# Threshold attention with a feed-forward block on one core: nine slots of 256 queries a batch, FFN by 288 tokens, scores in six shared PSUM banks, variance by a broadcast product

## Chip, cores, metric

One core of one Trainium2 chip. The metric is device time in microseconds (us) of one execution. The kernel before takes 1555.65 us, the median of 3 runs (1554.12 to 1557.59). Ratios are the mean time of one kernel's fast runs over that of the other's fast runs in the same rounds, so they are not quite the ratio of the medians quoted beside them; 95% intervals are in brackets.

The engines are called PE (TensorE; PEld its weight loads), DVE (VectorE), ACT (ScalarE), POOL (GpSimd) and SP (SyncE, which issues most transfers).

## The reference, cut

```python
# q, k, v: (8, 8, 576, 64) float32; tau = 0.02; w_ch1: 512 x 2048; w_ch2: 2048 x 512 (float64)
scores = np.matmul(q, k.transpose(0, 1, 3, 2)) / np.sqrt(64)
thresh = np.max(scores, -1, keepdims=True) - tau
scores = np.where(scores >= thresh, scores, -1e9)
attn   = softmax(scores)                       # (written out in the original)
x      = (attn @ v).transpose(0, 2, 1, 3).reshape(8, 576, 512)
mu, var = x.mean(-1), x.var(-1)                # per token
xn     = (x - mu) / np.sqrt(var + 1e-6) * g_ln
out    = x + np.maximum(xn @ w_ch1, 0) @ w_ch2
```

A *unit* below is one pair of heads of one batch. "em" is the transposed attention weights, "hidden" the output of the first FFN product after its ReLU, "o" an output tile of the second.

## The kernel before, what matters

All products are float32. A unit is worked off in five points: four of 128 queries of both heads, and one that holds the 64 queries of both that are left, through a block-diagonal stationary operand. Each side of a point has a PSUM tile of its own, from a pool that turns over two:

```python
scs = [ps_sc.tile([128, 2, 512], F32, tag="sc", name="sc") for _ in sides]   # ps_sc: bufs=2
...
for i, sc in enumerate(scs):                     # exponentials
    nc.vector.tensor_reduce(out=neg[:, i:i+1], in_=sc[:, :, :HALF], op=ALU.max, negate=True, ...)
    nc.gpsimd.tensor_scalar(out=thr[:, i:i+1], ...)
    nc.scalar.activation(es[:, i]..., sc[:, :, :HALF], func=AF.Exp, bias=neg[:, i:i+1])
...
for i, sc in enumerate(scs):                     # weights: multiply by (score >= threshold)
    nc.vector.scalar_tensor_tensor(out=e2, in0=sc[:, :, :HALF], scalar=thr[:, i:i+1], in1=e2, ...)
```

The FFN goes by nine groups of 512 tokens. Each output tile of it takes a PSUM bank of a pool of two, and ACT (first product) or DVE (second) empties it. The DVE multiply is put in a list, `aside`, which is issued after the point's threshold multiplies:

```python
for m in range(NK):
    p2 = ps_ff.tile([128, TOK], F32, tag="ff", name="p2")
    for d in range(ND):
        product(p2, lhsT=w2_sb[d][:, m*128:(m+1)*128], rhs=hidden[:, d], ...)
    aside.append(lambda m=m, p2=p2: add_to_x(g, m, p2, rb))    # o = p2 * rb, then + x
...
scs = scores(u, j);  es, thr = exponentials(scs);  conversion.carry()
run(3 * n);  second_part(n, 0)          # FFN products, a share of the open group
weights(scs, es, thr);  run_aside()
conversion.end();  run(3 * n + 1);  second_part(n, 1)
```

The float64 weights are turned into float32 on the fly in the first points (`conversion`): work for DVE, ACT and POOL.

Of the kernel before, what the change touches and what calls it, by code (L numbers as in the profile page):

```python
# [18 lines left out]
def kernel(  # L19
# [24 lines left out]

    nc = tc.nc
    B, H, S, D = q.shape
    DM = H * D
    DF = w_ch1.shape[1]
    assert (S, D, DM) == (576, 64, 512) and DF % 128 == 0
# [4 lines left out]
    PTS = J + 1  # L54
    NB = S // 32
    HALF = S // 2
    SCALE = 1.0 / 8.0
    BIG = 3.0e38
    TOK = 512
    NG = B * S // TOK  # L60
    assert NG * TOK == B * S

    consts = ctx.enter_context(tc.tile_pool(name="consts", bufs=1))
    ins = ctx.enter_context(tc.tile_pool(name="ins", bufs=2))
# [3 lines left out]
    xpool = ctx.enter_context(tc.tile_pool(name="xpool", bufs=3))  # L68
    ps_sc = ctx.enter_context(tc.tile_pool(name="ps_sc", bufs=2, space=bass.MemoryType.PSUM))
    ps_at = ctx.enter_context(tc.tile_pool(name="ps_at", bufs=2, space=bass.MemoryType.PSUM))  # L70
    ps_ff = ctx.enter_context(tc.tile_pool(name="ps_ff", bufs=2, space=bass.MemoryType.PSUM))

    ffn = ctx.enter_context(tc.tile_pool(name="ffn", bufs=4))
# [10 lines left out]
    q_diag = [consts.tile([128, 128], F32, name=f"q_diag{i}") for i in range(2)]  # L84
    v_rest = [consts.tile([128, 2, D], F32, name=f"v_rest{i}") for i in range(2)]
# [30 lines left out]
    def load_v(u):  # L116
        b, hp = units[u]
        vt = ins.tile([128, J, 2, D], F32, tag="v", name="v_in")
        vr = v_rest[u % 2]
        for h in range(2):  # L120
            nc.sync.dma_start(  # L121
                out=vt[:, :, h, :],
                in_=v[b, 2 * hp + h, : J * 128, :].rearrange("(c p) d -> p c d", p=128),
            )
            nc.sync.dma_start(out=vr[64 * h : 64 * h + 64, h, :], in_=v[b, 2 * hp + h, J * 128 :, :])  # L125
        values_in[u] = (vt, vr)
# [5 lines left out]
    for t in v_rest:  # L132
        nc.gpsimd.memset(t, 0.0)
    for t in q_diag:
        nc.gpsimd.memset(t, 0.0)
    load_qk(0, (nc.sync, nc.scalar))
# [19 lines left out]

    hidden = consts.tile([128, ND, TOK], F32, name="hidden")

    def weight_steps(which):
# [10 lines left out]
        if which == 1:  # L170
            chunks = [
                (w1_sb[i][:, c : c + WC], w_ch1[i * 128 : (i + 1) * 128, c : c + WC], i)
                for c in range(0, DF, WC)
                for i in range(NK)
            ]
        else:
            chunks = [
                (w2_sb[i], w_ch2[i * 128 : (i + 1) * 128, :], None) for i in range(ND)
            ]
        size = len(chunks)  # L180
        step = 4 if which == 1 else 2
        place = [ND - step * ((i % 4 if which == 1 or i < size - 4 else i % 2) + 1) for i in range(size)]
        raws, made = {}, {}

        def fetch_raw(i):
            at = place[i]
            raws[i] = hidden[:, at : at + 2].rearrange("p a n -> p (a n)").bitcast(I64)
            nc.sync.dma_start(out=raws[i], in_=chunks[i][1])

        def begin(i):  # L190
            if which == 1:
                a, y = hidden[:, place[i] + 2], hidden[:, place[i] + 3]
            else:
                a = ffn.tile([128, WC], F32, tag="o", name="w_bits")
                y = ffn.tile([128, WC], F32, tag="o", name="w_size")
            raw = raws.pop(i)
            words = raw.bitcast(U32).rearrange("p (n two) -> p n two", two=2)
            lo, hi = words[:, :, 0], words[:, :, 1]
            r = raw.bitcast(I32).rearrange("p (n two) -> p n two", two=2)[:, :, 0]
            au = a.bitcast(U32)  # L200
# [8 lines left out]
            nc.scalar.activation(r, lo, func=AF.Copy, scale=2.0**-29)  # L209
            nc.scalar.activation(  # L210
                y, raw.bitcast(F32).rearrange("p (n two) -> p n two", two=2)[:, :, 1],
                func=AF.Square,
            )
            made[i] = (a, y, r)

        def carry(i):
            a, y, r = made[i]
            ai = a.bitcast(I32)
            nc.gpsimd.tensor_tensor(out=ai, in0=ai, in1=r, op=ALU.add)
            if place[i] in place[i + 1 :]:  # L220
                fetch_raw(place.index(place[i], i + 1))

        def end(i):
            a, y, r = made.pop(i)
            dst, _, gi = chunks[i]
# [4 lines left out]
            if gi is not None:  # L230
# [3 lines left out]
                )  # L234

        return size, lambda: [fetch_raw(place.index(at)) for at in sorted(set(place), reverse=True)], begin, carry, end
# [5 lines left out]
    def turn(u):  # L242
# [4 lines left out]

        q_in, k_in = loaded.pop(u)
        qT = att.tile([128, J * 128], F32, tag="qT", name="qT")
        kT = att.tile([128, S], F32, tag="kT", name="kT")  # L250
        qd = q_diag[u % 2]
# [4 lines left out]
        if by_blocks(u):  # L256
            qr = qT.rearrange("p (r j a c) -> p r a j c", r=2, j=2, a=4)
            for r in range(2):
                nc.vector.transpose(  # L259
                    qr[:, r], q_in[:, 8 * r : 8 * r + 8].rearrange("p (a j) c -> p a j c", j=2)  # L260
                )
        else:
            nc.vector.transpose(qT, q_in[:, : J * 4].rearrange("p n c -> p (n c)"))
        for h in range(2):
            r = slice(64 * h, 64 * h + 64)
            nc.vector.transpose(qd[r, r], q_in[r, J * 4 :].rearrange("p n c -> p (n c)"))
        turned[u] = (qT, kT, qd)

    def scores(u, j):

        qT, kT, qd = turned[u]
        if j < J:
            sides = [
                (qT[h * 64 : (h + 1) * 64, j * 128 : (j + 1) * 128], slice(h * 64, (h + 1) * 64))
                for h in range(2)
            ]
        else:
            sides = [(qd, slice(0, 128))]
        scs = [ps_sc.tile([128, 2, 512], F32, tag="sc", name="sc") for _ in sides]
        for c in range(2):  # L280
            for sc, (lhsT, rows) in zip(scs, sides):
                (nc.tensor.matmul if j < J else product)(  # L282
                    sc[:, c, :HALF], lhsT=lhsT, rhs=kT[rows, c * HALF : (c + 1) * HALF],
                    start=True, stop=True,
                )
        return scs

    def exponentials(scs):

        neg = small.tile([128, 2], F32, tag="neg", name="neg")  # L290
        thr = small.tile([128, 2], F32, tag="thr", name="thr")
        es = att.tile([128, 2, S], F32, tag="e", name="e")
        for i, sc in enumerate(scs):
            nc.vector.tensor_reduce(  # L294
                out=neg[:, i : i + 1], in_=sc[:, :, :HALF], axis=AXL.XY, op=ALU.max, negate=True
            )
            nc.gpsimd.tensor_scalar(  # L297
                out=thr[:, i : i + 1], in0=neg[:, i : i + 1], scalar1=-1.0, scalar2=low_sb,
                op0=ALU.mult, op1=ALU.add,
            )  # L300
            nc.scalar.activation(  # L301
                es[:, i].rearrange("p (c n) -> p c n", c=2), sc[:, :, :HALF],
                func=AF.Exp, bias=neg[:, i : i + 1],
            )
        return es, thr

    def weights(scs, es, thr):

        n = len(scs)
        den = small.tile([128, 2], F32, tag="den", name="den")  # L310
        for i, sc in enumerate(scs):
            e2 = es[:, i].rearrange("p (c n) -> p c n", c=2)
            nc.vector.scalar_tensor_tensor(  # L313
                out=e2, in0=sc[:, :, :HALF], scalar=thr[:, i : i + 1], in1=e2,
                op0=ALU.is_ge, op1=ALU.mult, accum_out=den[:, i : i + 1],
            )
        nc.vector.reciprocal(den[:, :n], den[:, :n])  # L317
        for i in range(n):
# [5 lines left out]
    rounds = {}  # L324

    def turn_weights(u, j, es):


        if j in (0, 2, 4):
            n = 256 if j < J else 64  # L330
            em = att.tile([128, 2, J, 256], F32, tag="em", name="em")
            er = att.tile([128, 256], F32, tag="er", name="er")
            rounds[u] = (em, er, n)
        em, er, n = rounds[u]
        tr = ps_at.tile([128, 2, 128], F32, tag="at", name="tr")
        for h in range(2):
            e = es[:, h] if j < J else es[:, 0]
            if j < J or h == 0:
                pool, tag = (ps_at, "at") if h == 0 else (ps_ff, "ff")
                tp = pool.tile([128, J, 128], F32, tag=tag, name="tp")  # L340
                for c in range(J):
                    nc.tensor.transpose(tp[:, c], e[:, c * 128 : (c + 1) * 128], ident)
                if j < J:
                    o = (j % 2) * 128
                    nc.scalar.copy(em[:, h, :, o : o + 128], tp)
                else:
                    nc.scalar.copy(
                        em[:, :, :, :64], tp.rearrange("p c (h t) -> p h c t", h=2)
                    )
            if h == 0:  # L350
                nc.tensor.transpose(tr[:64, 0], e[:, 512:576], ident)
            else:
                nc.tensor.transpose(tr[:, 1], e[:, 448:576], ident)
# [368 lines left out]
```

## Time and profile before

The span is 1552.0 us. These are the page's engine line for PE, its row of granted clock in 40 slices (9 is 90% or more of full speed), and the view of what TensorE waited for (us in all, times, longest).

```profile
PE 1441.3 (93%) x8208; PEld 603.6 (39%) x8208; DVE 815.9 (53%) x1538; ACT 421.6 (27%) x762; POOL 498.6 (32%) x757
...
PEclk9888799999999999999999999999999999999999
```

```profile
PE pv L421 <- DMA em<-scr: 29.4, 24, 3.0
PE pv L421 <- ACT em L345: 20.8, 7, 5.5
PE sc L282 <- DVE e L313: 15.3, 10, 2.6
...
PE p L95 <- ACT hidden L506: 4.4, 16, 0.6
```

TensorE is the bound: 93% busy, and only 111 us of the span are not (1552.0 - 1441.3). The clock is below 9 in slices 2 to 5 only. FFN products hardly ever wait for the ReLU that empties their bank: 4.4 us in all.

| | before |
|---|---|
| median, us | 1555.65 |
| PE busy / idle, us | 1441.3 / 110.7 |
| mean granted clock | 0.973 |
| waits of values for the fetched transposes | 29.4 us |
| waits of FFN for ReLU | 4.4 us |

### The profile page before, as it was taken

Reading aid. Unit: us, or ns where it says so; the run is one execution under the profiler, and the core shown is the slowest. Engines: PE = TensorE matmul, PEld = TensorE weight load, DVE = VectorE, ACT = ScalarE, POOL = GpSimd, SP = SyncE. Lnnn points to the kernel's source line nnn. Section 1 sums busy time; section 2 is a strip of 40 time slices with the busy share of each in tenths; the row PEclk is TensorE's granted clock in tenths of the full one; section 3 lists DMA queues with packets and bytes.
Section 4 is the critical chain, followed back from the end, with each engine's and each line's share of the span. In section 5 each row is a group of like instructions: output and inputs, shape, how many; then the busy total and the mean of one; then the engine's idle time right before and its main releaser. Section 6 shows DMA issues by size and latency. Waiting matters only on the chain.

```text
span 1552.0 us, 22825 instructions
## 1 busy us (share of the span) xinstructions
PE 1441.3 (93%) x8208; PEld 603.6 (39%) x8208; DVE 815.9 (53%) x1538; ACT 421.6 (27%) x762; POOL 498.6 (32%) x757
## 2 busy tenths in 40 slices
PE   4666789989999999999999999999999999999998
PEld 3444234433443443344443444434433444333332
DVE  6777975656566555655566556656656551011001
ACT  3655442213321242123212321143113320210200
POOL 5676642333233323332233323332333232100000
PEclk9888799999999999999999999999999999999999
DMA  7443677777677777777777777777776665001001
GB/s 147 99 128 83 161 184 160 166 166 157 150 156 169 165 151 159 161 167 160 160 162 149 165 156 163 162 159 161 161 161 156 139 147 120 8 5 16 7 7 21
DMA packets 701471, 204.68 MB, mean 132 GB/s; under 512 B 632752, under 2 KB 697264, under 8 KB 701360
## 3 DMA queue, kind: packets, MB, share of 16 engines
q1 hardware_dynamic: 698960, 202.95, 59.2%
q8 instruction: 65, 1.06, 0.3%
q10 hardware_dynamic: 2368, 0.30, 0.2%
q14 instruction: 46, 0.38, 0.1%
q0 software_dynamic: 32, 0.00, 0.0%
HBM read 119.41 MB, written 83.76 MB: 131 GB/s over the span
## 4 chain that ended last, share of the span: by engine, by line
PE 77%; DMA 7%; DVE 6%; SPq 6%; ACT 2%; issue 2%; POOL 1%; POOLq 0%; ACTq 0%; DVEq 0%
PE p L95 56%; PE pv L421 11%; PE sc L282 7%; DMA em<-scr 6%; PE sc L95 2%; SPq L484 2%; DVE neg L294 2%; DVE e L313 1%; ACT e L301 1%; SPq L377 1%; SPq L125 1%; SPq L107 1%; ACT hidden L506 1%; SPq L403 1%; SPq L121 1%
## 5 line engine op out<-in xcount | busy, mean ns | idle before, releaser
L95 PE MATMUL p<-xc,w 128*64 128x512 f32 x2304 | 519.4, 596 | 11.4 <-DVE xc L460 7.0
L95 PE MATMUL p<-hidden,w 128*64 128x512 f32 x2304 | 513.4, 593 | 0.0
L294 DVE TENSOR_REDUCE neg<-sc 128x1 f32<-128x576 f32 x288 | 206.0, 752 | 329.2 <-PE sc L282 268.2
L301 ACT ACTIVATE e<-sc,neg 128x576 f32<-128x576 f32 x288 | 199.9, 739 | 604.9 <-DVE neg L294 598.7
L319 POOL TENSOR_SCALAR e<-e,den 128x576 f32<-128x576 f32 x288 | 232.1, 812 | 226.4 <-DVE den L317 209.0
L95 PEld LDWEIGHTS p<-xc,w 128*64 128x64 f32 x2304 | 172.6, 137 | 301.8 <-issue 273.9
L95 PEld LDWEIGHTS p<-hidden,w 128*64 128x64 f32 x2304 | 169.9, 137 | 300.2 <-issue 289.3
L313 DVE SCALAR_TENSOR_TENSOR e<-sc,thr,e 128x576 f32<-128x576 f32 x288 | 225.5, 816 | 76.2 <-ACT e L301 72.1
L297 POOL TENSOR_SCALAR thr<-neg,low_sb 128x1 f32<-128x1 f32 x288 | 76.2, 265 | 530.8 <-DVE neg L294 527.0
L421 PE MATMUL pv<-em,v_in 128*64 128x256 f32 (+1 forms) x1536 | 171.7, 351 | 59.4 <-DMA em<-scr 29.4
L282 PE MATMUL sc<-kT,qT 64*128 64x288 f32 x1024 | 173.1, 443 | 25.2 <-DVE e L313 15.3
L506 ACT ACTIVATE hidden<-p 128x512 f32<-128x512 f32 x144 | 86.1, 598 | 345.1 <-PE p L95 345.1
L370 DVE STREAM_TRANSPOSE et<-e 128x1152 f32<-128x1152 f32 x112 | 153.0, 1366 | 0.5
L421 PEld LDWEIGHTS pv<-em,v_in 128*64 128x64 f32 x1536 | 96.1, 142 | 136.2 <-issue 41.5
L282 PEld LDWEIGHTS sc<-kT,qT 64*128 64x128 f32 x1024 | 96.3, 192 | 134.7 <-issue 101.0
L476 POOL TENSOR_TENSOR o<-o,x 128x512 f32<-128x512 f32 x36 | 45.8, 1272 | 215.5 <-DVE o L475 215.5
L475 DVE TENSOR_TENSOR o<-p,rb 128x512 f32<-128x512 f32 x36 | 24.6, 684 | 162.0 <-PE p L95 150.6
L421 PE MATMUL pv<-er,v_rest 128*64 128x256 f32 (+1 forms) x384 | 60.0, 338 | 0.0
L432 ACT COPY x<-pv 128x256 f32<-128x256 f32 (+3 forms) x120 | 32.2, 290 | 94.0 <-PE pv L421 91.5
L515 POOL TENSOR_TENSOR ss<-ss,sq 128x512 f32<-128x512 f32 x27 | 34.5, 1277 | 65.3 <-ACT sq L513 65.3
L259 DVE STREAM_TRANSPOSE qT<-q_in 128x256 f32<-128x256 f32 x56 | 21.5, 423 | 44.5 <-POOL q_in L252 44.4
L460 DVE TENSOR_TENSOR xc<-x,mean 128x512 f32<-128x512 f32 x36 | 22.2, 679 | 27.8 <-PE mean L95 27.8
(62 smaller groups left out, 631.4 us busy)
## 6 DMA issues: line engine op xcount, KB each, us to landing
scr<-et SPq DMA_DIRECT2D x224, 288.0 KB, 5.4
em<-scr SPq DMA_DIRECT2D x112, 512.0 KB, 5.1
hidden<-in_moe_w_ch_dram SPq DMA_DIRECT2D x32, 512.0 KB, 4.0
q_in<-in_q_dram SPq DMA_DIRECT2D x128, 72.0 KB, 4.9
out_dram<-ot SPq DMA_DIRECT2D x144, 64.0 KB, 2.0
k_in<-in_k_dram SPq DMA_DIRECT2D x124, 72.0 KB, 3.3
v_in<-in_v_dram SPq DMA_DIRECT2D x64, 128.0 KB, 3.5
scr_rest<-et SPq DMA_DIRECT2D x112, 72.0 KB, 4.5
```

Of the source, the lines that this page charges most:

```text
L95: nc.tensor.matmul(out[r], lhsT=lhsT[:, r], rhs=rhs, **flags)
L282: (nc.tensor.matmul if j < J else product)(sc[:, c, :HALF], lhsT=lhsT, rhs=kT[rows, c * HALF : (c + 1) * HALF], start=True, stop=True,)
L294: nc.vector.tensor_reduce(out=neg[:, i : i + 1], in_=sc[:, :, :HALF], axis=AXL.XY, op=ALU.max, negate=True)
L297: nc.gpsimd.tensor_scalar(out=thr[:, i : i + 1], in0=neg[:, i : i + 1], scalar1=-1.0, scalar2=low_sb, op0=ALU.mult, op1=ALU.add,)
L301: nc.scalar.activation(es[:, i].rearrange("p (c n) -> p c n", c=2), sc[:, :, :HALF], func=AF.Exp, bias=neg[:, i : i + 1],)
L313: nc.vector.scalar_tensor_tensor(out=e2, in0=sc[:, :, :HALF], scalar=thr[:, i : i + 1], in1=e2, op0=ALU.is_ge, op1=ALU.mult, accum_out=den ...
L319: nc.gpsimd.tensor_scalar(out=es[:, i], in0=es[:, i], scalar1=den[:, i : i + 1], scalar2=1.0, op0=ALU.mult, op1=ALU.mult,)
L370: nc.vector.transpose(et[:, :, :, j % 2], es.rearrange("p h (n c) -> p h n c", c=32))
L421: nc.tensor.matmul(pv[64 * h : 64 * h + 64, :n], lhsT=vt[:, c, h, :] if c < J else vr[:, h, :], rhs=em[:, h, c, :n] if c < J else er[:, :n ...
L476: nc.gpsimd.tensor_tensor(out=o, in0=o, in1=groups[g][:, m], op=ALU.add)
L506: nc.scalar.activation(hidden[:, d], p1, func=AF.Relu)
L515: nc.gpsimd.tensor_tensor(out=ss, in0=ss, in1=sq, op=ALU.add)
```

## The change

The intent: fewer and larger pieces of attention (nine slots a batch, each 256 queries of two heads, which is twice a point), the second half of the batch one stage behind the first, so that an FFN group of 288 tokens is ready after half a batch; a whole slot of time for the round trip of the transposed weights; six of eight PSUM banks as one tile for scores, with the values in a free corner of it; variance by one product that gives every partition the sum, without the small transposes. The core of the diff:

```diff
-    HALF = S // 2
+    TOK = S // 2                       # 288
+    QH = 256
+    SLOTS = 2 * HP + 1                 # 9
+    NG = 2 * B                         # 16 groups
...
+    sc = ps_sc.tile([128, 6 * 512], F32, name="sc")
+    pv = sc[:, 1024 + 128 : 1024 + 128 + QH]
...
-        for i, sc in enumerate(scs):
+        for i in (0, 2):
             nc.vector.tensor_reduce(
-                out=neg[:, i : i + 1], in_=sc[:, :, :HALF], axis=AXL.XY, op=ALU.max, negate=True
+                out=neg[:, i : i + 2], in_=sc[:, block(i) : block(i) + 2 * S].rearrange("p (j n) -> p j n", j=2), axis=AXL.X, op=ALU.max, negate=True
             )
...
+        for i in range(4):
+            nc.scalar.activation(es[:, i], blocks[i], func=AF.Exp, bias=neg[:, i : i + 1])
...
-            if d == 10:
-                rp = ps_ff.tile([128, TOK // 128, 128], F32, tag="ff", name="rp")
...
+                var = ps_ff.tile([128, TOK], F32, tag="ff", name="var")
+                product(var, lhsT=avg_sb, rhs=sq[:, 0], start=True, stop=True)
+                nc.scalar.activation(rb, var, func=AF.Sqrt, bias=eps_sb)
+                aside.append(lambda: nc.vector.reciprocal(rb, rb))
...
+        tick(0)                        # a step of the weight conversion
+        run(n, -1)                     # values of an earlier slot
+        scores(b, s)
+        es, thr = exponentials()
+        tick(1)
+        run(n, 0)
+        second_part(n, 0)              # FFN, first quarter
+        run(n, 1)
+        second_part(n, 1)
+        weights(es, thr)
+        run_aside()                    # multiplies of finished second-product tiles
```

## The prediction

> **What bounds the kernel now.** I read the windows of the span first, then the groups of instructions by line, then the timeline of TensorE in the middle, then the waits of TensorE. The windows (us, then busy us of PE, PEld, DVE, ACT, POOL, then clock, DMA share, GB/s) show three stages:
>
> ```profile
> 80.00:120.00 40.00, 27.65 (x184) 17.82 (x184) 29.90 (x61) 22.13 (x49) 28.64 (x35) 0.83 0.40 115
> 640.00:800.00 160.00, 155.12 (x918) 65.46 (x916) 92.55 (x175) 41.35 (x71) 50.12 (x84) 1.00 0.73 160
> 1400.00:1500.00 100.00, 99.48 (x480) 33.69 (x478) 4.39 (x7) 12.34 (x22) 7.61 (x6) 1.00 0.05 9
> ```
>
> From about 170 us on, TensorE is 97 to 100% busy at full clock, and no other engine reaches 60%. The timeline of the middle shows that this is real streaming, not waiting:
>
> ```profile
> 703.40 1.24 PE L282 MATMUL sc<-kT,qT 64*128 64x288 f32 x8
> 704.57 0.69 PE L421 MATMUL pv<-em,v_in 128*64 128x64 f32 x16
> ...
> 710.36 1.14 PE L95 MATMUL sc<-kT,q_diag 128*64 128x288 f32 x8
> 711.33 3.60 PE L95 MATMUL p<-xc,w 128*64 128x512 f32 x16
> ...
> 738.30 0.60 PE L421 MATMUL pv<-er,v_rest 128*64 128x256 f32 x4
> 738.73 4.46 PE L95 MATMUL p<-xc,w 128*64 128x512 f32 x20
> ```
>
> Starts give the true cost. The product of diagonal queries, 288 columns, takes 711.33 - 710.36 = 0.97 us for 8 records, that is 0.485 us for a product (4 records). An FFN product of 512 columns takes 0.857 us (weight loads come in pairs every 0.43 us). Scores of one old point take 704.57 - 703.40 = 1.17 us, the values of 256 queries 1.78 + 0.43 = 2.21 us. The first FFN product starts only at 168.9 us; the batch of attention before it is a latency chain over DVE, ACT and POOL with weight conversion between. Of 1552 us, I count some 1380 us of work and 172 of loss: about 115 in the opening, 27 where values wait for a fetched transpose (22.8 between 320 and 1280), 24 in switches and small waits, 7 at the end. Only loss can be won.
>
> **What the Trainium skill says.** "TensorE: Matmul & The Clock Gate", Back-to-back issue gap: about N/2.4 ns for N columns; the trace agrees (512 columns: 0.214 us a record, 288: 0.121). So cutting 512 to 288 tokens costs nothing by itself. Its Part 1 says the clock halves when a whole idle window of some 3.4 us passes; the opening agrees: values after a gap of 3.75 us took 3.68 us, after 2.27 us 1.95. "ScalarE: Activation LUTs", What ACT_TABLE_LOAD costs: 186 or 280 ns plus 0.833 ns an element; the trace's exp of 576 has 739 ns, its ReLU of 512 598, so a ReLU of 288 should take 0.41 us (estimate). "PSUM — Partial Sum Buffer", Engine vs sequencer instructions: ScalarE's and VectorE's queues are strictly in order; no reordering shows in the trace.
>
> **The change part by part.**
>
> *FFN:* 16 x 128 products x 0.485 = 993 us against 9 x 128 x 0.857 = 987. Mean and variance: 32 x 0.485 = 15, about as before. *Scores:* pieces of 512, 64, 448, 128 columns; the same columns, small pieces perhaps bounded by weight loads: 2.48 us a slot (estimate, 2 x 1.17 plus 0.14), 4.0 the shared slot. *Values and transposes:* the same work. So TensorE's work stays at 1380 to 1385 us.
>
> *Won:* the fetch of a slot's transposed weights has a whole slot of slack now, so the 27 us should go. The FFN starts after seven slots instead of 24 points.
>
> *A new wait, for the copy of the values.* Scores and values now lie in one PSUM tile. In the compiled program the first score matmul of a slot waits for ScalarE's copy of the values issued just before it, and the values come before the scores. From the opening: the values' last issue is over at 71.83, the copy runs 72.11 to 72.48, so TensorE stands about 0.7 us. Times 70 slots: 49 us.
>
> *A new wait, for ReLU behind the exponentials.* The same tile makes the first of four exponentials wait for both reduces, and the first threshold multiply wait for all four. ScalarE's order after a slot's scores is four exponentials, then the ReLUs of the FFN products that TensorE starts at once:
>
> ```profile
> 706.31 1.42 DVE L294 TENSOR_REDUCE neg<-sc 128x1 f32<-128x576 f32 x2
> ...
> 707.16 1.37 ACT L301 ACTIVATE e<-sc,neg 128x576 f32<-128x576 f32 x2 [4.20 <-DVE neg L294]
> ...
> 721.38 1.28 ACT L301 ACT_TABLE_LOAD   x1 [1.33 <-DVE neg L294]
> ```
>
> Two reduces over two blocks take about 2.7 us, four exponentials 2.7, one ReLU 0.41: with latencies the first bank is free 6.05 us after the scores. Before, exponentials ended 2.3 us after the scores and a hidden tile lasted 3.43. Now TensorE has two FFN banks, and a hidden tile of 288 tokens lasts 4 x 0.485 = 1.94 us. The compiled order gives what is left of the open tile at each slot's start: in a batch, five slots are in the first FFN product, with 3.9, 1.9 (the variance takes the second bank), 3.4, 3.9 and 2.4 us of work before the third bank is needed. The third and fifth also hold an exponential's table load (1.28). Stalls: 2.1 + 4.1 + 3.9 + 2.1 + 4.9 = 17 us a batch, 118 over batches 1 to 7.
>
> *Opening.* Slots 0 to 2 are one chain: cold scores 5, reduces 2.7, exponentials 2.9, multiplies 3.3, normalizing on GpSimd 4.4, conversion 2.1, scaling of queries 0.7, their transposes 1: 22 us each. Slots 4 to 6, with five conversions, whose GpSimd and DVE parts alternate: about 23. FFN begins near 155 us. In slots 7 to 9 an open FFN tile leaves one bank to five transposes with a copy each; 30 us a slot. The scores of slot 10 start at about 260 by this walk; I take 250, since some of it must overlap.
>
> *Sum.* From slot 10: FFN 1943 x 0.485 = 942, mean and variance 15, scores 55 x 2.48 + 7 x 4.0 = 164, values 57 x 2.21 + 7 x 2.52 = 144, copies 63 x 0.7 = 44, ReLU 118, switches 17, last store 6: 1450. With 250: **1700 us**.
>
> **The rivals.**
> (1) *TensorE stays the only bound and the waits are smaller than I think*: with neither new wait, the sum is 1450 - 162 + 250 = 1538, and with an opening 40 us shorter, 1498. For it: the FFN starts earlier in program order and the intent is plainly less idling. Against it: both waits stand in the compiled program, and the durations are measured.
> (2) *The waits bite harder*: gaps of 4 to 5 us in the middle sometimes cover a whole idle window, and the clock halves for a few us; two or three such a batch would add 10 to 60 us, 1710 to 1760. Against: the middle of before holds 1.00.
> (3) *DMA or the single buffers of fetched weights become the bound*: the share was 0.73 with the same bytes in a batch; a batch gets longer, not shorter, so I give it no time.
> (4) *The opening is won as intended* (FFN from 120 us): minus 35 us, 1665.
>
> **Range and chances.** The spread comes from the ReLU stalls (118, by a third), the opening (by 35) and the clock: 1630 to 1765. For a gain of 2% (below 1525) both new waits would have to be nearly absent and the opening shorter: 3%. Within 2% (to 1587) the stalls would have to be a third of my count: 6%. Slower: 91%.
>
> **What will show it.** TensorE's waits: scores for the copy of the values (x from sc), near 70 times 0.7 us; FFN products for ScalarE's ReLU, some 35 to 40 times 2 to 5 us, just after scores; hardly any wait of values for em. FFN records spaced at 0.121 us. Starts of reduce, exponential and multiply strictly one after the other. A batch of nine slots near 196 us (256 x 0.485 + 2 + 23.8 + 20.2 = 170 of work, 17 of ReLU, 6 of copies, 3 of switches). If scores do not wait for the copy, or the first-product slots last no longer than the second-product slots, my main steps are wrong; if slots 0 to 9 take under 220 us, the opening is.

## The result, and the profile after

The changed kernel takes **1831.26 us** (median of 4 runs, 1830.6 to 1832.01), beside 1556.62 of the kernel before in the same rounds: ratio 1.175 [1.170, 1.180]. It is slower, as predicted, and by more: 131 us over the predicted 1700, outside the range of 1630 to 1765.

The same three views of the changed kernel:

```profile
PE 1489.3 (81%) x11704; PEld 862.9 (47%) x11704; DVE 818.2 (45%) x1380; ACT 444.7 (24%) x810; POOL 476.7 (26%) x735
...
PEclk7777789899999999999999999999999999999999
```

```profile
PE p L99 <- ACT hidden L567: 105.1, 35, 4.5
PE tp L380 <- ACT em L389: 51.7, 14, 7.9
PE mean L99 <- DVE o L534: 50.5, 8, 6.4
PE sc L326 <- ACT x L494: 37.4, 52, 10.8
PE sc L326 <- DVE qT L278: 31.9, 4, 14.8
PE p L99 <- DVE o L534: 30.5, 6, 5.1
```

TensorE is busy 48 us longer than before with the same multiplications, DVE, ACT and POOL within 25 us of before; idle time of TensorE went from 111 to 340 us (1829.6 - 1489.3). Waits for the fetched transposes are gone from the list, which was the aim. In their place stand two waits that the kernel before did not have: products of the first FFN layer for the ReLU (105.1 us), and products and means for the DVE multiply o that empties a bank of the second layer (50.5 + 30.5 = 81.0 us). The waits for tp and qT, and 15 of the 37 us of the copies x, lie before 290 us, in the opening.

One stall of each kind, in the timeline of TensorE (start, duration, output and inputs, number of records, in brackets what it waited for):

```profile
909.26 1.90 PE L478 MATMUL sc<-em,v_in 128*64 128x256 f32 x16
910.99 0.60 PE L478 MATMUL sc<-er,v_rest 128*64 128x256 f32 x4
912.09 2.33 PE L326 MATMUL sc<-kT,qT 64*128 64x512 f32 x16 [0.50 <-ACT x L494]
914.35 4.10 PE L99 MATMUL p<-hidden,w 128*64 128x288 f32 x32
918.28 0.66 PE L99 MATMUL mean<-sum,avg_sb 128*64 128x288 f32 x4
924.02 10.11 PE L99 MATMUL p<-hidden,w 128*64 128x288 f32 x64 [5.09 <-DVE o L534]
...
939.02 4.10 PE L99 MATMUL p<-xc,w 128*64 128x288 f32 x32
944.93 5.31 PE L99 MATMUL p<-xc,w 128*64 128x288 f32 x42 [1.81 <-ACT hidden L567]
```

And what ACT and DVE did meanwhile, one fence each:

```profile
917.27 2.63 ACT L347 ACTIVATE e<-sc,neg 128x576 f32<-128x576 f32 x4 [5.23 <-DVE neg L339]
```

```profile
914.53 2.62 DVE L339 TENSOR_REDUCE neg<-sc 128x2 f32<-128x1152 f32 x2 [4.97 <-PE sc L326]
920.01 0.82 DVE L354 SCALAR_TENSOR_TENSOR e<-sc,thr,e 128x576 f32<-128x576 f32 x1 [2.85 <-ACT e L347]
...
923.55 0.42 DVE L534 TENSOR_TENSOR o<-p,rb 128x288 f32<-128x288 f32 x1
```

One shared chain: two reduces (914.53 to 917.15), only then four exponentials (to 919.90), only then four threshold multiplies (to 923.0), and behind them the multiply at 923.55 that frees the bank TensorE has lacked since about 918.9. That multiply takes 0.42 us, and its tile was complete at about 918.3. It stood in DVE's queue behind four multiplies that it has nothing to do with, and those waited for ACT. The kernel before issues it behind the threshold multiplies too, and has no such wait. My reading, which no run tests alone: a second-product tile took 16 x 0.857 = 13.7 us there and takes 16 x 0.485 = 7.8 us here, so a bank is wanted back sooner, while a slot has four threshold multiplies instead of two in front.

The 64 records after the gap took 10.11 us; the same 64 without a gap took 7.98 in a kernel of the first experiment below. The windows tell why (us; busy us of PE, PEld, DVE, ACT, POOL with instructions; then granted clock, DMA share, GB/s):

```profile
912.00:918.00 6.00, 5.91 (x46) 3.50 (x48) 2.62 (x2) 0.77 (x3) 1.26 (x3) 1.00 0.77 154
918.00:924.00 6.00, 0.93 (x8) 0.29 (x4) 3.96 (x12) 1.90 (x4) 0.64 (x1) 0.80 0.62 114
924.00:928.00 4.00, 3.98 (x18) 2.04 (x20) 4.00 (x7) 0.00 (x0) 3.75 (x6) 0.50 0.68 210
928.00:932.00 4.00, 4.00 (x34) 2.25 (x32) 2.12 (x6) 0.00 (x0) 0.00 (x0) 0.95 0.91 216
```

The clock column reads 1.00, then 0.80 as the gap goes on, 0.50 when the work resumes, and 0.95 four us later: the gap of 5.1 us costs another 2.1 us after it (10.11 - 7.98).

| | before | after |
|---|---|---|
| median, us | 1556.62 | 1831.26 |
| PE busy / idle, us | 1441.3 / 110.7 | 1489.3 / 340.3 |
| mean granted clock | 0.973 | 0.920 |
| FFN for ReLU / for the multiply o, us | 4.4 / 0 | 105.1 / 81.0 |
| waits for em from the DMA, us | 29.4 | 0 |

### The profile page after: what moved, and what is told of

It reads as the page before. It is cut to its first block, busy times and chain, and to the rows that moved or that the text cites. A ratio compares the mean times of both kernels' runs of the same rounds, so it can differ in the third digit from the quotient of the medians.

```text
span 1829.6 us, 29170 instructions
## 1 busy us (share of the span) xinstructions
PE 1489.3 (81%) x11704; PEld 862.9 (47%) x11704; DVE 818.2 (45%) x1380; ACT 444.7 (24%) x810; POOL 476.7 (26%) x735
## 4 chain that ended last, share of the span: by engine, by line
PE 69%; DVE 11%; ACT 10%; issue 4%; POOL 2%; DMA 2%; SPq 2%; ACTq 0%; DVEq 0%; POOLq 0%
PE p L99 49%; PE sc L326 8%; PE sc L478 8%; DVE neg L339 8%; ACT e L347 6%; DVE e L354 2%; PE sc L99 2%; ACT x L494 1%; ACT L347 1%; POOL e L360 1%; ACT hidden L567 1%; DMA er<-scr 1%; SPq L111 1%; DMA stage<-in_moe_w_ch_dram 1%; PE tp L380 1%
## 5 line engine op out<-in xcount | busy, mean ns | idle before, releaser
L99 PE MATMUL p<-xc,w 128*64 128x288 f32 x4096 | 533.4, 419 | 80.4 <-ACT hidden L567 79.0
L99 PE MATMUL p<-hidden,w 128*64 128x288 f32 x4096 | 547.7, 429 | 56.7 <-DVE o L534 30.5
L99 PEld LDWEIGHTS p<-hidden,w 128*64 128x64 f32 x4096 | 309.5, 145 | 283.7 <-issue 40.2
L99 PEld LDWEIGHTS p<-xc,w 128*64 128x64 f32 x4096 | 296.4, 141 | 303.2 <-ACT hidden L567 98.5
L339 DVE TENSOR_REDUCE neg<-sc 128x2 f32<-128x1152 f32 x144 | 188.8, 1353 | 411.5 <-PE sc L326 339.1
L354 DVE SCALAR_TENSOR_TENSOR e<-sc,thr,e 128x576 f32<-128x576 f32 x288 | 218.3, 815 | 212.8 <-ACT e L347 212.7
L326 PE MATMUL sc<-kT,qT 64*128 64x512 f32 (+3 forms) x1024 | 161.2, 457 | 83.0 <-ACT x L494 37.4
L567 ACT ACTIVATE hidden<-p 128x288 f32<-128x288 f32 x256 | 102.6, 416 | 305.0 <-PE p L99 305.0
L478 PE MATMUL sc<-em,v_in 128*64 128x256 f32 (+1 forms) x1536 | 144.9, 333 | 0.0
L478 PEld LDWEIGHTS sc<-em,v_in 128*64 128x64 f32 x1536 | 94.0, 140 | 44.0 <-issue 3.6
L535 POOL TENSOR_TENSOR o<-o,x 128x288 f32<-128x288 f32 x64 | 51.0, 796 | 226.1 <-DVE o L534 226.1
L380 PE MATMUL tp<-ident,e 128*128 128x128 f32 x144 | 31.4, 379 | 57.8 <-ACT em L389 51.7
```

Source lines behind the costliest of these rows:

```text
L99: nc.tensor.matmul(out[r], lhsT=lhsT[:, r], rhs=rhs, **flags)
L326: nc.tensor.matmul(sc[:, at : at + n], lhsT=qT[r, half, j * 128 : (j + 1) * 128], rhs=kT[r, o : o + n], start=True, stop=True,)
L339: nc.vector.tensor_reduce(out=neg[:, i : i + 2], in_=sc[:, block(i) : block(i) + 2 * S].rearrange("p (j n) -> p j n", j=2), axis=AXL.X, op ...
L354: nc.vector.scalar_tensor_tensor(out=es[:, i], in0=blocks[i], scalar=thr[:, i : i + 1], in1=es[:, i], op0=ALU.is_ge, op1=ALU.mult, accum_o ...
L380: nc.tensor.transpose(tp[:, c], es[:, i, c * 128 : (c + 1) * 128], ident)
L478: nc.tensor.matmul(dst[64 * h : 64 * h + 64], lhsT=vt[:, c, h, :] if c < J else vr[:, h, :], rhs=rhs, start=(c == 0), stop=(c == J),)
```

## The experiments

There were fifteen runs, all correct but one, each timed in 3 rounds beside the kernel before. Differences between two kernels below are differences of medians; the kernel before had medians of 1556 to 1561 us in all those rounds (which ran on two chips), so a few us between runs of different rounds mean nothing. The theory after the result: the time is lost in two orders within ScalarE's and VectorE's queues, which are long because one tile makes scores' readers wait for one another, plus the clock that the gaps cost. The main rival: the smaller FFN tiles and larger slots themselves cost it.

### mul_first: the freeing multiply ahead of the threshold multiplies

```diff
-            aside.append(lambda m=m, p2=p2: add_to_x(g, m, p2, rb))
+            muls.append(lambda m=m, p2=p2: add_to_x(g, m, p2, rb))
...
         second_part(n, 0)
+        run_muls()
         run(n, 1)
```

> Edit: the multiply that empties a finished second-product bank is issued on VectorE before the four threshold multiplies of the slot, not after them. Theory (the changed kernel's waits are serial losses of TensorE, and gaps of 4 us and more also halve its clock for a while): the 81 us in which TensorE waited for the multiply o (mean 50.5, products 30.5) fall under 15, and the time falls by these and some 20 to 30 us of clock, to 1715 to 1760. Rival (the wait only hides the next one, the bound being the chain of a slot): the waits move to the ReLU or the scores and the time stays over 1800.

Measured: 1747.70 us, ratio to before 1.120 [1.117, 1.123], so 84 us less than the changed kernel. The waits of TensorE:

```profile
PE p L99 <- ACT hidden L575: 105.1, 35, 4.5
PE tp L380 <- ACT em L389: 53.1, 14, 7.9
```

The wait for o is gone and the ReLU wait has not moved, to the tenth. As the theory expected, but for the clock: TensorE is busy 15 us less (1474.6), not 20 to 30, and waits for fetched transposes come back with 6.9 us.

### relu_first: the FFN's first quarter, with its ReLU, ahead of the exponentials

```diff
-        es, thr = exponentials()       # reduces and exponentials
-        tick(1)
-        run(n, 0)
-        second_part(n, 0)
+        es, thr, neg = exponentials()  # reduces alone
+        second_part(n, 0)
+        exps(es, neg)
+        tick(1)
+        run(n, 0)
```

> Edit: the first quarter of FFN products of a slot is issued before the four exponentials, so that its ReLUs stand ahead of them in ScalarE's queue. Theory: the 105 us in which TensorE waited for ReLU fall under 25; with the clock that comes back the time is 1690 to 1745. Rival (bound is the slot's chain): exponentials now start up to 2 us later, the slot is as long, the time stays over 1800.

Measured: 1718.88 us, ratio 1.101 [1.098, 1.104], 112 us less than the changed kernel. The mirror image of the run before:

```profile
PE mean L99 <- DVE o L536: 50.8, 8, 6.7
...
PE p L99 <- DVE o L536: 30.5, 6, 5.1
PE p L99 <- ACT hidden L569: 20.3, 14, 2.0
```

ReLU's wait fell from 105.1 to 20.3, and the wait for o stayed (50.8 + 30.5). So these are two waits with two causes.

### values_after: the values product after the scores

```diff
-        run(n, -1)
-        scores(b, s)
+        scores(b, s)
+        run(n, -1)
```

> Edit: the values are multiplied after the slot's scores instead of before, so no score waits for ScalarE's copy. The waits of scores for the copy, 0.5 us each in the steady part (30 us), go; the reduces then wait for values and copy, about 0.3 us later in relation to the FFN than now, which lengthens the 35 ReLU waits by some 10 us. Theory: 1800 to 1818. Rival (the copy stands for more than its wait, because every slot's gap there costs clock): below 1780.

Measured: 1853.85 us, ratio 1.188 [1.184, 1.190]. A miss: 22 us slower where 13 to 31 less were expected. The scores no longer wait for a copy, but:

```profile
PE p L99 <- ACT hidden L567: 120.7, 35, 5.0
PE tp L380 <- ACT em L389: 61.0, 14, 13.9
PE mean L99 <- DVE o L534: 54.7, 8, 6.9
```

```profile
PEclk7676888889999898898998899998988989998999
```

The long gaps grew by about half a us each (the one at 925.91 is 5.58 us instead of 5.09), the mean clock fell from 0.920 to 0.891, and PE's busy time rose from 1489.3 to 1520.4. A wait taken away ahead of a longer one only moves into the longer one, and here it made that one cost more clock. The loss is in TensorE's busy time: from slot 10 to the end it is busy 1365.6 us instead of 1328.9, for nearly the same number of records (10698 and 10676), and idle 7 us less; slot 10 itself starts 7 us sooner (271.38 us).

### split_tile: the six score banks as two tiles of three

```diff
-    sc = ps_sc.tile([128, 6 * 512], F32, name="sc")
+    sides = [ps_sc.tile([128, 3 * 512], F32, name=f"sc{i}") for i in range(2)]
```

> Edit: the six score banks are two PSUM tiles of three instead of one. Nothing else moves. Theory (the one tile makes exponentials wait for both reduces and multiplies for all four exponentials): the first exponential starts 1.4 us after the first reduce starts instead of 2.7, ScalarE is free for the ReLU about 1.3 us sooner, and the 35 waits for ReLU shrink by 1.3 each, 45 us, with the multiplies and so the o waits 1.3 us sooner too (14 waits, 18 us): 1750 to 1785. Rival (dependencies are by region and the chain is serial for another reason): 1831 within 10.

Measured: 1692.48 us, ratio 1.084 [1.082, 1.087]: 139 us less, more than expected (46 to 81). The same offsets in the code and the same instructions; only what waits for what differs. What the threshold multiplies on DVE waited for, first the changed kernel's group of instructions (busy us, mean ns, idle just before them), then the view of waits of this kernel:

```profile
L354 DVE SCALAR_TENSOR_TENSOR e<-sc,thr,e 128x576 f32<-128x576 f32 x288 | 218.3, 815 | 212.8 <-ACT e L347 212.7
```

```profile
DVE e L357 <- ACT e L350: 33.9, 67, 1.6
```

And the waits of its TensorE:

```profile
PE p L99 <- ACT hidden L570: 46.1, 35, 3.2
...
PE mean L99 <- DVE o L537: 30.3, 8, 4.2
...
PE p L99 <- DVE o L537: 15.1, 6, 2.5
```

Threshold multiplies waited 212.7 us for exponentials and now 33.9, so both waits of the FFN are shorter together: 105.1 to 46.1 and 81.0 to 45.4, 95 us. The rest of the 139 is clock (0.920 to 0.949, 27 us of busy time) and the opening (tp 51.7 to 38.1). My expectation counted the shorter chain once and not the clock.

### relu_mul and relu_mul_split: both orders, without and with the two tiles

> Both orders at once: the multiply that empties a finished second-product bank issued before the threshold multiplies (alone 84 us off) and the walk's first quarter, with its ReLU, issued before the four exponentials (alone 112 us off). Theory that the two waits are different waits (ReLU on ScalarE 105 us, multiply on VectorE 81 us) and that each gap of 4-5 us costs its clock besides: the gains add, 1620 to 1655 us, ReLU wait near 20 us, waits for o under 10 us, clock about 0.955. Rival, that the two sit in one chain (reduce, exponentials, multiplies) and removing one lets the other grow: 1685 to 1720 us, with a new wait of over 40 us in the same slots.

Measured: 1624.18 us, ratio 1.044 [1.040, 1.047], 207 us less than the changed kernel where the two alone gave 84 + 112 = 196. The mean clock is 0.963, and the waits for ReLU and for o are:

```profile
PE p L99 <- ACT hidden L577: 21.1, 16, 2.0
...
PE mean L99 <- DVE o L544: 0.2, 1, 0.2
```

The gains add; the 11 us beyond that are not shown, since the ratios, each against the kernel before of its own round, give about 205 for both and 201 for the sum.

> The same two orders and the six score banks as two tiles of three (alone 139 us off). Theory that splitting the tile shortens the very same two waits (the chain through the exponentials gets shorter, so ReLU and o come earlier): the gains overlap, and this run is only 20 to 50 us under the run with both orders, 1580 to 1625 us. Rival, that the split removes something else as well (waits of the scores in the opening, clock): 1530 to 1575 us.

Measured: 1588.59 us, ratio 1.021 [1.018, 1.024], 36 us below relu_mul: inside the 20 to 50 of the theory that the split works on the same waits. So the split alone was worth 139 us and after both orders 36.

### three_split: the values after the scores once more

The edit of values_after on top of relu_mul_split.

> As the run before it, and the values product issued after the scores instead of before. Alone this change lost 22 us, by my reading because the 0.5 us gaps it took away were put into the 5 us gaps and lowered the clock. Theory: with the long gaps gone, the copy waits (47 x 0.5 us in the steady part) are a plain gain, 15 to 35 us under the run with scores last, and the clock does not fall. Rival: the values product is of use where it stands (it covers the end of the multiplies before the scores need the banks), and this run is the same or slower by up to 25 us, with a wait of the scores or of the reduces in its place.

Measured: 1564.47 us, ratio 1.005 [1.003, 1.007], 24 us below relu_mul_split. The edit that lost 22 us alone wins 24 here, and the waits for copies are gone for good. The mean clock of the profiled run is 0.959 (0.972 without the edit; 0.959 to 0.966 and 0.966 to 0.972 over all four runs of each), so it fell a little, which the theory had denied; the low slices are those of the opening. In the middle:

```profile
800.00:960.00 160.00, 155.21 (x1308) 91.13 (x1306) 83.52 (x138) 46.39 (x84) 45.24 (x76) 0.99 0.60 144
```

For the same stretch of the changed kernel:

```profile
800.00:960.00 160.00, 136.79 (x1118) 79.30 (x1115) 75.34 (x134) 35.47 (x65) 41.08 (x68) 0.95 0.54 128
```

TensorE does 1308 records in 160 us instead of 1118, at clock 0.99. This is the answer to the rival: a kernel with slots of 256 queries, FFN tiles of 288 and a shared corner for the values is within 0.5% of the kernel before, so they are not where the 275 us went. What each of them costs alone was not tested.

### before_var: the variance alone

In the kernel before, the sum of squares goes through one product by the averaging matrix; square root and reciprocal work on the whole tile.

```diff
-                var = ps_ff.tile([128, TOK // 128], F32, tag="ff", name="var")   # four products of 1 column
...
-                    nc.tensor.transpose(rp[:, i], rstd[:, i : i + 1].to_broadcast([128, 128]), ident)
+                var = ps_ff.tile([128, TOK], F32, tag="ff", name="var")
+                product(var, lhsT=avg_sb, rhs=ss, start=True, stop=True)
+                nc.scalar.activation(rb, var, func=AF.Sqrt, bias=eps_sb)
+                aside.append(lambda: nc.vector.reciprocal(rb, rb))
```

> The kernel before with one part of the change alone: the variance by one broadcast product over all 512 tokens, square root and reciprocal on the full 128x512 tile, in place of four one-column products, a small reciprocal and four transposes. Theory: TensorE work is within 1 us a group and the longer reciprocal (3 to 3.5 us nine times on VectorE, worked out from the 1.94 us of the 288-column one) lies off the path, so the same within 0.5 per cent, 1550 to 1568 us. Rival: the long reciprocal stands ahead of threshold multiplies and costs its length each time, up to 30 us more.

Measured: 1564.76 us, ratio 1.005 [1.002, 1.008]. Inside the expected range: this part of the change is not where the time went. It is not free, though: 0.5%, just clear of noise. DVE's busy time rose by 27 us (815.9 to 842.5), and waits of values for fetched transposes read 38.7 us instead of 29.4 (one trace each). Whether the long reciprocal delays those transposes, a small form of the rival, is not shown.

### after_slack: a looser weight conversion, in the changed kernel

```diff
-        tick(0)
-        run(n, -1)
+        run(n, -1)
+        tick(0)
...
-            if self.ended < self.carried:
+            if self.ended < self.carried - (1 if self.begun < len(self.chunks) else 0):
                 self.end()
```

> The changed kernel with its conversion loosened only: a chunk of weights is ended one tick later than now (GpSimd's part gets a whole tick of time before VectorE asks for it), and the first tick of a slot follows the copy of values in ScalarE's queue instead of standing before it. Theory on the opening: slots 4 to 6 take 27.8 us each because ticks chained at 3.3 us hold VectorE, and the copy of values waits behind them for 10 us twice; loosened, those slots fall to 20 to 23 us, slot 10 starts near 260 instead of 278, and the time falls by 12 to 25 us to 1806 to 1820 us. Rival, that the opening is bound by the sum of VectorE's and GpSimd's work and not by the chain: slot 10 starts at 272 or later and the time falls by under 8 us.

Measured: 1843.85 us, ratio 1.185 [1.182, 1.188]: 13 us slower. A miss, of theory and rival both. Slot 10's scores start at 273.69 us instead of 278.00, which the rival had (272 or later); then this is given back, since FFN products wait for weights that are ended later (10.7 us, 6.6 of it before 290 us, a wait that is new) and slot 11 starts at 302.20 us as before (302.31). By then TensorE has done 164 records fewer (996 against 1160): the FFN is behind, and from slot 11 on TensorE is busy 20 us longer (1330.8 against 1310.7) and idle 8 less. The loosened ticks gained 4 us at slot 10 and cost the FFN its start.

### open_q, open_slack, open_both: the opening, on top of three_split

open_q puts the scaling of the next unit's queries ahead of the four normalisations in POOL's queue; open_slack is the edit of after_slack (here it also puts the slot's first tick behind its scores); open_both has both.

```diff
+        if turning:
+            scale(u)                   # nc.gpsimd.tensor_scalar on q_in, until now in turn(u)
         weights(es, thr)               # with the four normalisations on POOL
...
             turn(u)
```

> The kernel with all four edits (scores first, both orders, two tiles; 1564 us), and the scaling of the next unit's queries put ahead of the four normalisations in GpSimd's queue instead of behind them. In the opening the scores wait 33.5 us in four waits for the turned queries, and the turn waits 11.4 us for that scaling. Theory: 10 to 16 us off, 1548 to 1555 us, wait for the turned queries under 20 us. Rival: the loads of weights or the conversion take its place: within 4 us of the run without it.

Measured: **1551.24 us** (1549.31 to 1551.38), ratio 0.9965 [0.9938, 0.9993], 13 us below three_split; the scores' wait for the turned queries fell from 33.5 to 21.7 us (the theory said under 20). This is the fastest kernel, and faster than the kernel before by a third of a per cent, which is no practical gain. Its page:

```profile
PE 1421.9 (92%) x11704; PEld 840.8 (54%) x11704; DVE 815.3 (53%) x1380; ACT 444.8 (29%) x810; POOL 479.8 (31%) x735
...
PEclk9877999999999999999999999999999999999999
```

> The kernel with all four edits and the loosened conversion (ended one tick later; first tick of a slot after the values). There VectorE waits 16.8 us for GpSimd's part of a tick between 75 and 145 us. Theory: 10 to 20 us off, 1545 to 1555 us. Rival, FFN now starts without its weights because the conversion ends later: 0 to 10 us slower.

Measured: 1592.75 us, ratio 1.024 [1.021, 1.027]. A miss beyond what the rival had, 28 us slower than three_split.

> All four edits, the earlier scaling of the queries and the loosened conversion together. Theory: the two act in different slots (0 to 3, and 4 to 6) and add, 1530 to 1545 us, 1 to 2 per cent under the kernel before. Rival, one bound (the conversion of 32 chunks) sets the opening whatever is moved: no better than the better of the two, about 1550 us.

Measured: 1580.81 us, ratio 1.016 [1.013, 1.018]. A miss. The scaling is worth 12 us here too, and the loosened conversion costs 28 to 30 wherever it is added to these four edits: it keeps the FFN waiting for weights (8.9 us in open_slack; slot 7 of open_slack starts at 158.71 us, that of three_split at 152.26). By slot 11, which starts 13 us later (271.56 against 258.38), TensorE has done 165 records fewer (976 against 1141), and the stretch from there to the end is 14 us longer, in which TensorE is busy 14 us more.

### after_noconv, after_q, open_ticks: what the opening consists of

after_noconv is wrong (relative error 0.74): the conversion is one short DVE operation a chunk, all else in place. after_q is the edit of open_q alone in the changed kernel.

```diff
-            nc.scalar.activation(both(I32)[:, :, 0], both(U32)[:, :, 0], func=AF.Copy, scale=2.0**-29)
-            nc.scalar.activation(y, both(F32)[:, :, 1], func=AF.Square)
...                                     # and 2 operations of POOL, 2 more of DVE
```

> Wrong on purpose: the changed kernel with the weight conversion reduced to one short VectorE operation a chunk (loads, places and ticks unchanged; the result is wrong), so that ScalarE's two operations, GpSimd's two and two of VectorE's three are gone. Theory: the sum of the conversion's work on those three engines is what makes slots 3 to 9 long; slot 10 then starts at 225 to 245 us instead of 278, the rest of the run is as it was, and the time falls by 30 to 55 us. Rival: the chain of a slot without an FFN to fill it (scores, reduces, exponentials, multiplies, transposes on two banks) sets the opening: slot 10 at 265 or later, under 15 us off.

Measured: 1789.78 us, ratio 1.147 [1.143, 1.150], 41 us less; slot 10 starts at 236.73 us instead of 278.00. As the theory had it (225 to 245). From 40 to 160 us, the changed kernel and then this one:

```profile
40.00:160.00 120.00, 62.87 (x388) 40.61 (x389) 73.35 (x130) 53.11 (x100) 70.06 (x78) 0.70 0.29 81
```

```profile
40.00:160.00 120.00, 82.48 (x568) 51.84 (x568) 51.54 (x110) 41.76 (x84) 33.32 (x54) 0.79 0.38 112
```

No engine is full in either, so I take it that a chain through DVE, ACT and POOL is what gets shorter. The steady waits are as in the changed kernel (ReLU 103.3 us after 290), so the opening is a separate account.

> The changed kernel with the scaling of the next unit's queries moved ahead of the normalisations in GpSimd's queue, nothing else. With four other edits this was worth 13 us. Theory: slots 0 to 3 are bound by that one queue order, so the same 10 to 15 us here, slot 10 near 266 us, time 1815 to 1822 us. Rival: in this kernel the values' copy and the shared score tile take its place: under 6 us.

Measured: 1821.24 us, ratio 1.167 [1.164, 1.170], 10 us less, slot 10 at 268.83 us. At the lower edge of the theory.

In open_ticks the ticks of open_q are moved forward:

```diff
-        ticks = (0, 2) if n < 4 else range(5)
+        ticks = (0, 2, 3) if n < 4 else (0, 1, 2, 3) if n < 6 else range(5)
```

> The best kernel so far (all four edits and the earlier scaling, 1551 us) with the conversion's ticks moved forward: three instead of two in slots 0 to 3, four instead of five in slots 4 and 5. Theory that engines are idle in slots 0 to 3 and full in 4 to 6: 5 to 12 us off, 1539 to 1546 us. Rival: slots 0 to 3 get as much longer as the others get shorter: within 4 us.

Measured: 1565.52 us, ratio 1.003 [1.000, 1.006], 14 us slower than open_q (10 by the ratios): a miss. Slot 4 starts at 85.24 us instead of 65.60, and slots 4 and 5 win nothing like that back (slot 6 at 123.63 instead of 103.82). Here a tick more in the first slots lengthened them, though their engines had idle time.

## Why the prediction was wrong

The direction, and four of its steps, held; the sum was 131 us short. The step that failed is its list of waits after slot 10: it lacks the second product's banks (81 us), and the clock that long gaps cost (about 50 us) stood in a rival and not in the sum. A further 28 us are the opening, which was taken and not derived. Two waits that were counted too large hide 27 us of the miss, by luck.

**TensorE's work stays the same: right.** Once the waits are gone (open_q) TensorE is busy 1421.9 us, 19 less than before; FFN products of 288 columns keep the predicted pace (32 records in 3.93 us, 914.35 to 918.28).

**Won, the wait for fetched transposes: right.** It is nought in the changed kernel. It comes back as 6.9 us in mul_first and 13.0 in relu_mul, when slots get shorter.

**The copy of the values: right in kind, too large in size.** The sum had 63 x 0.7 = 44 us; the trace has 30 us after 290 us, at 0.5 us each. 14 us too many.

**ReLU behind the exponentials: right.** 118 us predicted, 105.1 in 35 waits measured; relu_first showed the cause. 13 us too many. (Its five stalls make 17.1 us a batch and so 120 over seven, not 118.)

**Missing in the sum: the second product's banks.** The list has the banks that ReLU empties and none for those that the multiply o empties, though the prediction knew that DVE works in order and that its four threshold multiplies come late. Its test, that slots of the first product last longer than those of the second, was too blunt to tell: in the batch from 703.70 us the slots of the first product lasted 21.2 to 27.6 us, and two of the second with a wait for o (5.08 and 6.41 us) lasted 24.8 and 23.4. Measured: 81.0 us; mul_first takes them away and wins 84. The question that finds it is "who empties this bank, and what stands before that instruction in its engine's queue?", and it was asked of one of the two engines.

**The clock, left in a rival.** Rival 2 gave clock losses 10 to 60 us and stayed outside the sum, because the middle of before holds 1.00. But after 290 us before has no wait over 2.9 us, so that was no evidence. After slot 10 the kernel took 1831 - 278 = 1553 us against 1450 predicted: 103 too few. The missing wait makes 81 of it, the two that were too large take back 27, so some 49 us are left over. From slot 10 to the end, in the changed kernel and then in open_q, which has no long gaps there:

```profile
278.00:1829.60 1551.60, 1328.88 (x10676) 764.82 (x10676) 672.51 (x1129) 339.30 (x617) 357.39 (x590) 0.95 0.49 117
224.88:1547.50 1322.62, 1276.74 (x10698) 751.84 (x10696) 669.40 (x1129) 339.64 (x618) 359.72 (x590) 0.99 0.57 137
```

For nearly the same number of records TensorE is busy 52 us longer, at the lower clock. Single gaps agree with that, two of them from the batch that starts at 703.70:

```profile
783.55 9.44 PE L99 MATMUL p<-hidden,w 128*64 128x288 f32 x76 [3.72 <-ACT hidden L567]
...
873.29 11.61 PE L99 MATMUL p<-xc,w 128*64 128x288 f32 x80 [4.54 <-ACT hidden L567]
```

At 0.1217 us a record (104 in 12.66 us, from 797.87 to 810.53) the 76 lost nothing and the 80 lost 1.7 us; after the gaps of 5.08 and 6.41 us the loss was 2.2 and 2.0. That is 6 us a batch, 42 over seven. (Of two gaps of 3.72 us, here and one batch later, the second cost 1.7 us.) The batch took 208.4 us and not 196. The runs agree too (mean clock 0.920, 0.941, 0.936, 0.963 as the waits go).

**The opening: taken, not derived.** The walk gave 260 for slot 10 and the text took 250 "since some of it must overlap"; 278 was measured. Slots 0 to 2 took 19.1 to 20.6 us instead of 22, but slots 4 to 6 27.9, 27.8 and 25.9 instead of 23, and slots 7 to 9 34 to 38 instead of 30. after_noconv shows that the conversion makes 41 us of these 278, after_q the queue order of one POOL instruction 9. The falsifier, under 220, was not met. What sets slots 7 to 9 (still 34 to 35 us each without conversion) is settled in part: of their 109.5 us TensorE is idle 31, and 28 of these it waits for ACT's copies that empty the transposes' bank. The longest waits (7.7 us from 170 us on) are the same fault once more, since the copy (178.40 us) stands in ACT's queue behind the four exponentials (174.78 to 177.41) and two operations of the conversion. The clock is 0.77 to 0.82 there.

The text's reading of the kernel before is off in one place that the sum does not use: TensorE is not 97 to 100% busy from 170 us on but from about 240 (81% from 160 to 200 us, 90% to 240), and DVE is 95% busy from 160 to 200.

So 1700 + 28 (opening) + 81 (o) - 27 (copies, ReLU) + 49 (clock and what is left) = 1831.

**Where the intended gain went.** With all the queue orders mended (open_q), TensorE is busy 19 us less than before and idle 15 us more (125.6 against 110.7). In the first 290 us it is idle 83 us against 73 before, so the opening did not get shorter; between 290 us and the last group it is busy 96.9% of the time against 97.5%: the wait for the fetched transposes is won there, and 18 us of ReLU, 11 of turned queries and 5 of means are waited for in its place.

## What to carry to other kernels

When PSUM banks for a stream of products are few, list for each kind of tile the instruction that frees it and everything that its engine's queue holds ahead of it; issue the freeing instruction before work that waits for something else. A tile was a unit of waiting in this program (139 us in split_tile), so put buffers that have different readers in different tiles. Count each gap of about 5 us in an otherwise busy TensorE some 2 us longer than it is (1.7 to 2.2 in the batch above), and judge a small gain from removing a short wait only after the long ones are gone: the same edit lost 22 us and then won 24.

## What the Trainium skill lacked or had wrong

- "Perfetto Trace Analysis", Matmuls, advises to rotate through different banks so that emptying one overlaps the next group's products. The changed kernel does rotate two banks and still waited 186 us; how early the emptying instruction stands in its engine's queue was worth 207 us (relu_mul). The page says nothing on that.
- No page that I read says that readers of separate banks wait for one another when the banks are allocated as one tile; split_tile, with the same banks and instructions, was 139 us faster.
- "TensorE: Matmul & The Clock Gate", Part 1, states when the clock halves, and the trace agrees (0.50 in the four us after a gap of 5.09 us). It has no measured cost of a single gap in an engine that is over 80% busy: here 2.1 us for that one, 1.7 to 2.2 for three gaps of 4.5 to 6.4, and a mean clock of 0.920; half a us more a gap took it to 0.891.
- No page has a duration for VectorE's float32 reciprocal: 1.94 us for 288 columns, where a multiply of the same size that reads PSUM takes 0.44.
